# The second batch's phi softmax is moved ahead of the expert's pick, and its transposes go to other PSUM banks

## The chip, the cores and the metric

The kernel runs on one core of a Trainium2 chip. A core has a matrix engine (TensorE, PE in the profile, with its weight loads shown apart as PEld), a vector engine (VectorE, DVE), a scalar engine (ScalarE, ACT), GpSimd (POOL) and a sync engine (SyncE, SP) which here issues nearly all loads from HBM. Each engine takes its own instructions in the order in which the program lists them. The metric is the device time of one execution in microseconds (us), lower is better, and the median of the runs counts.

## The reference

Eight batches (B) of 576 tokens (S) with 8 heads (H) of 64 go through an attention in which keys and values are first gathered into 32 memory slots by a softmax over `phi`. The result is then sent through a mixture of 8 experts: each token picks one expert by a cosine with the expert's embedding.

```python
a = phi - np.max(phi, axis=2, keepdims=True)
a = np.exp(a)
a = a / (np.sum(a, axis=2, keepdims=True) + 1e-09)     # over the tokens
k_m = np.einsum('bhsm,bhsd->bhmd', a, k)
v_m = np.einsum('bhsm,bhsd->bhmd', a, v)
scores = scale * np.matmul(q, k_m.transpose(0, 1, 3, 2))
attn = softmax(scores)                                  # over the 32 slots
x = np.matmul(attn, v_m)                                # then (B*S, H*D)
...
expert_idx = np.argmax(xn @ en.T / tau, axis=1)
for e in range(E):
    mask = expert_idx == e
    h = np.maximum(x[mask] @ w1[e], 0.0)
    out[mask] = gate_w[mask, None] * (h @ w2[e])
```

## The kernel before

A batch has one expert for almost all of its tokens, so the kernel chooses one expert for the whole batch, loads its `w1` and `w2` and runs the 576 tokens through them as dense products; tokens with another expert would be done at the end. For batch 0 the expert is guessed early from the summed keys and values (`summed`, `guess`, `pick`), so that its weights can be loaded while the attention is still at work.

The function `moe_linformer` writes the start of the program out by hand: the attention of batch 0 and the gathering of batch 1 are mixed, line by line, and the order of these lines is the order in which each engine takes its instructions. Only then do the batches run in a loop (`batch`), whose stages `first` and `second` are the two products of the expert. A helper call such as `k.largest(1, 0)` therefore is at the same time a place in the queue of VectorE.

The 8 heads of a batch lie in two groups of four, g = 0 and g = 1. These are the steps around the change:

- `load_phi(1, (g,))` loads group g of batch 1's phi, 288 KB, into `ex`. SP issues it among the other loads.
- `largest(1, g)` (L509) takes the maximum over the tokens on VectorE, into `nm`. `softmax(1, (g,))` (L524) takes the exponential in place on ScalarE, with the sum in `sm`, and GpSimd copies the last 64 tokens apart (L526).
- `turn(1, g)` transposes four blocks of 128 tokens on TensorE into a PSUM tile `te` (L550) and copies them to `eT` on ScalarE (L551). `tails(1)` does the same with the last 64 tokens (`tz`, L557 and L558). `slots(1)` then multiplies `eT` with keys and values (`acc`, L607).
- `values(0)` transposes batch 0's values into a PSUM tile `tv` (L667) and copies them on ScalarE in four pieces (L673). `squares(0)` needs these copies; its result `tl` (L694) is copied by `products(0)` (L732).
- `score(0, tr, ...)` and `score(0, te, ...)` are batch 0's scores (`tr`, `te`, L686). VectorE transposes them into `x` (`fill`, L65), takes their maximum (`weigh`, L72) and subtracts it (L74, on GpSimd for g = 0), ScalarE takes the exponential (L76), VectorE sums (L85, `divide`), divides (L92) and transposes them back (L100, `aw`). With `aw` TensorE begins the attention's last product (`po`, L135), and from there the expert's first product (`pg`, L766, and `ph`, L791).
- `pick` (L227 to L231) reads the guess on VectorE and hands the expert's number to SP, which then issues the loads of `w1` (L494).

PSUM tiles come from named banks: `pt` takes the next of three in turn, `mm(..., n)` takes bank `m` with the number n. A new tile in a bank waits until the last reader of the tile before it is done. `warm` issues matmuls without use (`hot`, `warm0` to `warm2`), which keep TensorE at work.

Of the kernel before, what the change touches and what calls it, by code (L numbers as in the profile page):

```python
# [19 lines left out]
P = 128  # L20
# [27 lines left out]
class Tokens:  # L48
# [47 lines left out]
    def turn(self, gs, ks):  # L96

        k, nc, b = self.k, self.nc, self.b
        for g in gs:
            nc.vector.transpose(k.aw[:, g, 32 * ks.start : 32 * ks.stop], k.x[:, g, ks])  # L100
            if ks.stop == BL:
                nc.vector.transpose(k.aw[:, g, S:], k.x[:, g, BL - 2 :])  # L102
# [205 lines left out]
class Kernel:  # L308
# [234 lines left out]
        rs, g = self.room(b)[2], slice(gs[0], gs[-1] + 1)  # L543
        self.nc.vector.reciprocal(out=rs[:, g], in_=rs[:, g])

    def turn(self, b, g):

        t = self.pt([P, 4, P], f"te{b}_{g}")
        for k in range(4):
            self.nc.tensor.transpose(t[:, k], self.e(b, g)[:, P * k : P * k + P], self.ident)  # L550
        self.nc.scalar.copy(self.eT[:, 4 * g : 4 * g + 4], t)  # L551
# [558 lines left out]
@with_exitstack  # L1110
def moe_linformer(ctx, tc, phiT, qT, kv, kvt, emb, tau, w1, w2, out):
    k = Kernel(ctx, tc, phiT, qT, kv, kvt, emb, tau, w1, w2, out)
    ctx.enter_context(tc.manual_schedule(engines={ET.PE, ET.DVE, ET.Activation, ET.SP, ET.Pool}))


    k.eights()
    k.warm(8)
    k.warm(41, hot=k.mm([P, 64], "cool", 0))
    k.load_phi(0)
    k.load_kv(0)  # L1120
    k.load_q(0, (0,))
    k.load_router()
    k.consts()
    accs = [k.ps.tile([P, 2 * D], F32, tag=f"{n}3", name=f"acc0{n}", bufs=1) for n in "tm"]
    for vT in k.vT:
        k.nc.vector.memset(vT, 0.0)
    router = k.router()
    for g in range(NG):
        k.largest(0, g)
        k.softmax(0, (g,))  # L1130
    for g in range(NG):
        k.turn(0, g)
        if not g:
            next(router)
        k.warm(4 if g else 8, hot=k.mm([P, 256], f"half{g}", 0))
    k.tails(0)
    k.shares(0)
    next(router)
    k.load_phi(1, (0,))
    k.load_q(0, (1,))  # L1140
    k.load_phi(1, (1,))
    t = Tokens(k, 0, k.pt)
    for ks in ((0, 1), (4,), (2, 3)):
        k.slots(0, accs, ks=ks, first=0 in ks, last=3 in ks)
        if 3 not in ks:
            k.warm(3, hot=k.mm([P, 128], f"hot{ks[0]}", 0))
    k.scale(0)
    next(router, None)
    k.warm(2, hot=k.mm([P, 128], "hot2", 0))
    k.load_kv(1, (0,))  # L1150
    k.load_piece(1, 2)
    k.load_piece(1, 3)
    k.keys(0)
    t.summed()
    k.again()
    values = k.values(0, copy=k.nc.scalar.copy, room=lambda *a: k.mm(*a, 3))
    all, tr, te = slice(0, BL), [k.mm([P, S - 64], f"tr0_{g}", g) for g in range(NG)], [k.mm([P, 64], "te0_0", 2)]
    k.score(0, tr, 64, S, (0,))
    t.guess()
    k.score(0, te, 0, 64, (0,))  # L1160
    next(values)
    k.largest(1, 0)
    k.softmax(1, (0,))
    e = t.pick()
    t.fill((0,), slice(2, BL), tr)
    t.fill((0,), slice(0, 2), te)
    list(values)
    k.load_w1(e, 0)
    k.load_w1(e, 1)
    k.load_q(1, (0,))  # L1170
    tl = [k.pt([P, D + E], f"tl0_{g}") for g in range(NG)]
    k.squares(0, tl)
    k.score(0, tr, 64, S, (1,))
    te.append(k.pt([P, 64], "te0_1"))
    k.score(0, te, 0, 64, (1,))
    k.products(0, copy=True)
    k.largest(1, 1)
    work = [t.weigh((g,), all, None if g else k.nc.gpsimd) for g in range(NG)]
    for _ in range(2):
        next(work[0])  # L1180
    t.fill((1,), slice(2, BL), tr)
    t.fill((1,), slice(0, 2), te)
    k.softmax(1, (1,))
    k.turn(1, 0)
    k.warm(8, hot=k.mm([P, 256], "warm0", 3))
    k.turn(1, 1)
    list(work[0])
    for _ in range(2):
        next(work[1])
    list(work[1])  # L1190
    k.warm(8, hot=k.mm([P, 256], "warm1", 2))
    k.tails(1)
    k.shares(1, v=k.nc.gpsimd, invert=False)
    accs = [accs[0], k.mm([P, 2 * D], "acc1", 3)]
    for ks in ((0,), (1,), (2,), (4,), (3,)):
        k.slots(1, accs, ks=ks, first=0 in ks, last=3 in ks)
    project = k.project(0, k.vT[0], apart=True)
    t.divide(range(NG), all, True, lambda: k.invert(1))
    k.tags, k.turns = 4, 3
    k.scale(1)  # L1200
    k.again(k.nc.scalar.copy)
    t.turn(range(NG), all)
    for g in range(NG):
        k.part(g, slice(0, HS), k.nc.gpsimd.tensor_copy)
    k.warm(6, hot=k.mm([P, 256], "warm2", 2))
    k.keys(1, lambda *a: k.mm(*a, 3))
    list(k.values(1, copy=k.nc.scalar.copy, room=lambda *a: k.mm(*a, 2)))

    def between():
        for _ in range(3):  # L1210
            next(project)

    t.attend(between)
    t.turned(0, 1)
    t.turned(4)
    k.load_w2(e)
    k.load_q(1, (1,))
    k.load_phi(2)
    k.second_part = project
    for b in range(B):  # L1220
        u = Tokens(k, b + 1, k.pt) if b < B - 1 else None
        left = k.batch(b, t, u)
        t = u
    k.rest(*left)
# [29 lines left out]
```

## Time and profile before

| what | value |
|---|---|
| median of 3 runs | 391.76 us (389.92 to 392.36) |
| time of the profiled execution | 391.72 us |
| its span, first to last instruction | 389.9 us |
| TensorE busy (matmuls) | 383.0 us, 98% of the span |
| VectorE, ScalarE, GpSimd busy | 242.8, 213.3 and 190.1 us |
| mean granted TensorE clock | 0.999 |

The profile is of one execution; 1.8 us of its time lie outside of the span. All times in the views count from the start of the span. A busy matmul row counts its latency too, so that TensorE's share says little of where it waits; that is told by the weight loads (PEld), whose rows name an idle time and what ended it.

### The profile page before, as it was taken

To read this page: it belongs to the slowest core of one execution; us is meant where nothing else is said; L and a number is where in the kernel's file an instruction comes from. 1 tells how busy PE (TensorE), PEld (TensorE's weight loads), DVE (VectorE), ACT (ScalarE), POOL (GpSimd) and SP (SyncE) were. 2 spreads that over 40 slices of the span, in tenths; PEclk is the share of its full clock that TensorE was granted. 3 is DMA by queue.
4 is the path that set the end of the run, shared out by engine and by line. 5 is a ranking of instruction groups with operands and counts; after the bars stand their busy time and mean duration, and the time that the engine had idled before them with its cause. 6 is when DMAs were issued, how large, how long until landed. Compare 5 with 4: busy or idle time off the path is not lost. (4 is left out here: it accounts for less than half of the span.)

```text
span 389.9 us, 10386 instructions
## 1 busy us (share of the span) xinstructions
PE 383.0 (98%) x3881; PEld 313.5 (80%) x3881; DVE 242.8 (62%) x800; ACT 213.3 (55%) x665; POOL 190.1 (49%) x234
## 2 busy tenths in 40 slices
PE   8899999999999999999999999999999999999995
PEld 6578888798787978889787987879787897879883
DVE  4678996679663798259872798538861696545000
ACT  5466634868494865666657685657641751145011
POOL 1166930695155923378152941559242871529300
PEclk9999999999999999999999999999999999999999
DMA  8999938994699937994499917995379306970011
GB/s 314 397 358 349 366 78 228 346 389 156 161 315 375 379 72 167 400 380 174 91 310 366 402 34 168 345 386 209 65 185 382 127 2 130 322 306 2 30 54 44
DMA packets 65591, 91.25 MB, mean 234 GB/s; under 512 B 40728, under 2 KB 45336, under 8 KB 63488
## 3 DMA queue, kind: packets, MB, share of 16 engines
q1 hardware_dynamic: 62160, 81.02, 61.9%
q0 software_dynamic: 2688, 8.26, 5.7%
q10 hardware_dynamic: 688, 1.26, 1.1%
q8 instruction: 32, 0.52, 0.6%
q14 instruction: 23, 0.19, 0.1%
HBM read 71.19 MB, written 19.33 MB: 232 GB/s over the span
## 5 line engine op out<-in xcount | busy, mean ns | idle before, releaser
L791 PE MATMUL ph<-aT,gh 128*128 128x288 f32 x512 | 103.1, 296 | 0.0
L831 PE MATMUL py<-wh,hh 128*128 128x512 f32 x256 | 100.9, 394 | 0.0
L831 PE MATMUL py<-wl,hh 128*128 128x512 f32 x256 | 99.8, 390 | 0.0
L831 PE MATMUL py<-wh,hl 128*128 128x512 f32 x256 | 99.7, 389 | 0.0
L756 POOL TENSOR_TENSOR wl<-w2s,wh 128x512 fp32r<-128x512 f32 x64 | 83.3, 1302 | 5.1
L791 PEld LDWEIGHTS ph<-aT,gh 128*128 128x128 f32 x512 | 81.8, 188 | 1.9 <-DVE hl L798 0.8
L791 PE MATMUL ph<-aT,gl 128*128 128x288 f32 x256 | 75.4, 294 | 0.0
L795 ACT ACTIVATE hh<-ph 128x224 fp32r<-128x224 f32 (+1 forms) x128 | 48.7, 387 | 33.7 <-PE ph L791 33.0
L798 DVE SCALAR_TENSOR_TENSOR hl<-ph,hh 128x224 fp32r<-128x224 f32 (+1 forms) x128 | 51.8, 417 | 23.4 <-ACT hh L795 16.9
L997 POOL DMA_DIRECT2D out_dram<-ys x28 | 16.3, 582 | 91.2 <-ACT ys L836 88.9
L836 ACT ACTIVATE ys<-py,gate 128x512 f32<-128x512 f32 (+1 forms) x40 | 25.7, 643 | 63.7 <-PE py L831 33.9
L831 PEld LDWEIGHTS py<-wh,hh 128*128 128x128 f32 x256 | 48.1, 188 | 11.1 <-issue 1.4
L831 PEld LDWEIGHTS py<-wh,hl 128*128 128x128 f32 x256 | 48.1, 188 | 10.2
L831 PEld LDWEIGHTS py<-wl,hh 128*128 128x128 f32 x256 | 48.1, 188 | 9.4
L791 PEld LDWEIGHTS ph<-aT,gl 128*128 128x128 f32 x256 | 48.0, 188 | 0.0
L775 DVE TENSOR_TENSOR gl<-pg,gh 128x512 fp32r<-128x512 f32 x32 | 20.0, 683 | 43.9 <-ACT gh L771 43.9
L755 POOL CAST wh<-w2s 128x512 fp32r<-128x512 f32 x62 | 41.3, 666 | 0.1
L746 POOL TENSOR_TENSOR aT<-aw,aT 128x576 fp32r<-128x576 f32 (+1 forms) x18 | 23.5, 1319 | 32.7 <-DVE aT L745 29.2
L584 ACT COPY eT<-xt 32x256 f32<-32x256 f32 x80 | 32.3, 404 | 1.4
L820 PE MATMUL py<-w2s,h 128*64 128x256 f32 x256 | 29.4, 382 | 0.0
L656 ACT COPY kv<-kt 32x64 f32<-32x64 f32 x96 | 23.3, 243 | 6.4 <-DVE kt L646 5.2
L820 PEld LDWEIGHTS py<-w2s,h 128*64 128x64 f32 x256 | 17.7, 137 | 10.7 <-DVE aw L102 2.1
(184 smaller groups left out, 474.3 us busy)
## 6 DMA issues: line engine op xcount, KB each, us to landing
kx<-kv SPq DMA_DIRECT2D x15, 1024.0 KB, 12.0
w2s<-w SPq DMA_DIRECT2D x28, 512.0 KB, 10.0
w1s<-w SPq DMA_DIRECT2D x28, 512.0 KB, 5.8
qt<-qT SPq DMA_DIRECT2D x14, 576.0 KB, 10.2
out_dram<-ys POOLq DMA_DIRECT2D x28, 256.0 KB, 6.4
ad<-aw SPq DMA_DIRECT2D x8, 576.0 KB, 12.4
td<-x SPq DMA_DIRECT2D x56, 72.0 KB, 2.2
ea<-td SPq DMA_DIRECT2D x7, 512.0 KB, 4.2
```

The source lines that it names most:

```text
L584: nc.scalar.copy(eT[to, :8, m].rearrange("p (g k) m -> p g k m", g=NG), xt[at, :, q : BL - 2 : 4])
L656: nc.scalar.copy(y, self.kt[32 * l : 32 * l + 32, g, h + 2 * i :: 2 - 4 * i])
L746: self.nc.gpsimd.tensor_tensor(out=al, in0=a, in1=ah.bitcast(F32), op=ALU.subtract)
L755: (copy or self.nc.scalar.copy)(h, x)
L756: self.nc.gpsimd.tensor_tensor(out=l, in0=x, in1=h.bitcast(F32), op=ALU.subtract)
L775: nc.vector.tensor_tensor(out=self.gl[:, g, f], in0=ps[g], in1=self.gh[:, g, f].bitcast(F32), op=ALU.subtract)
L791: nc.tensor.matmul(p, lhsT=w[:, g, fs], rhs=x[:, g, to], start=g == 0 and k == 0, stop=g == 1 and k == 2)
L795: nc.scalar.activation(self.hh[:, f, at], q, AF.Relu)
L798: nc.vector.scalar_tensor_tensor(out=self.hl[:, f, at], in0=q, scalar=0.0, in1=self.hh[:, f, at].bitcast(F32), op0=ALU.max, op1=ALU.subtract)
L820: nc.tensor.matmul(p[64 * j : 64 * j + 64], lhsT=self.h4[:, f], rhs=self.w2s[:, f, d * j : d * j + d], start=f == 0, stop=f == 7,)
L831: nc.tensor.matmul(p, lhsT=h[:, f, to], rhs=w[:, f], start=f == 0 and k == 0, stop=f == 7 and k == 2)
L836: nc.scalar.activation(y[:, :d], p, AF.Copy, scale=gate[:, i : i + 1])
```

## The change

`largest(1, 0)` moves up to stand right behind `keys(0)`, ahead of `summed`; `largest(1, 1)` and both exponentials of batch 1 (`softmax(1)`) move ahead of `pick` and of the rest of `values(0)`, which holds the four copies. `turn(1, 0)` moves ahead of `squares(0)` and takes bank m3, where `tv` lies; `turn(1, 1)` takes bank m2. `tails(1)` moves ahead of the second half of `weigh`. The unused matmuls change: two groups of 8 with 256 columns become one group of 15 with 64 columns behind `tails(1)`, and the group of 6 with 256 columns ahead of `keys(1)` becomes 8 with 192 columns.

```diff
-    def turn(self, b, g):
+    def turn(self, b, g, room=None):
 
-        t = self.pt([P, 4, P], f"te{b}_{g}")
+        t = (room or self.pt)([P, 4, P], f"te{b}_{g}")
...
     k.keys(0)
+    k.largest(1, 0)
     t.summed()
...
     next(values)
-    k.largest(1, 0)
-    k.softmax(1, (0,))
+    k.largest(1, 1)
+    k.softmax(1)
     e = t.pick()
...
     k.load_q(1, (0,))
+    k.turn(1, 0, lambda *a: k.mm(*a, 3))
     tl = [k.pt([P, D + E], f"tl0_{g}") for g in range(NG)]
     k.squares(0, tl)
     k.score(0, tr, 64, S, (1,))
...
     k.products(0, copy=True)
-    k.largest(1, 1)
     work = [t.weigh((g,), all, None if g else k.nc.gpsimd) for g in range(NG)]
...
     t.fill((1,), slice(0, 2), te)
-    k.softmax(1, (1,))
-    k.turn(1, 0)
-    k.warm(8, hot=k.mm([P, 256], "warm0", 3))
-    k.turn(1, 1)
+    k.turn(1, 1, lambda *a: k.mm(*a, 2))
     list(work[0])
+    k.tails(1)
     for _ in range(2):
         next(work[1])
     list(work[1])
-    k.warm(8, hot=k.mm([P, 256], "warm1", 2))
-    k.tails(1)
+    k.warm(15, hot=k.mm([P, 64], "warm1", 3))
...
-    k.warm(6, hot=k.mm([P, 256], "warm2", 2))
+    k.warm(8, hot=k.mm([P, 192], "warm2", 2))
```

On VectorE, this is the stretch from the scaling of batch 0's keys and values (`ks<-acc0t`) to the first maximum of the scores (`mx0_00`), before the change. `nm1` are the maxima of batch 1, `key0` to `ai` is the pick.

```order
L626 TENSOR_SCALAR ks_75<-acc0t_186,rs0_192 128x128
L212 TENSOR_TENSOR ve_336<-kv21_79,key_331 128x32
L661 COPY ks_75<-ks_75 128x2x64
L509 TENSOR_REDUCE nm1_354<-ex_69 128x1
L227 TENSOR_REDUCE key0_363<-key_331 128x8
L228 MAX top_360<-key0_363 128x8
L229 MAX_INDEX at_361<-top_360,key0_363 128x8
L230 TENSOR_SCALAR ai_362<-at_361 128x1
L65 STREAM_TRANSPOSE x_81<-tr0_0_339 128x512
L65 STREAM_TRANSPOSE x_81<-te0_0_341 128x64
L509 TENSOR_REDUCE nm1_354<-ex_69 128x1
L72 TENSOR_REDUCE mx0_00_410<-x_81 128x18
```

The same stretch of VectorE after the change:

```order
L626 TENSOR_SCALAR ks_75<-acc0t_186,rs0_192 128x128
L509 TENSOR_REDUCE nm1_331<-ex_69 128x1
L212 TENSOR_TENSOR ve_340<-kv21_79,key_335 128x32
L661 COPY ks_75<-ks_75 128x2x64
L509 TENSOR_REDUCE nm1_331<-ex_69 128x1
L227 TENSOR_REDUCE key0_366<-key_335 128x8
L228 MAX top_363<-key0_366 128x8
L229 MAX_INDEX at_364<-top_363,key0_366 128x8
L230 TENSOR_SCALAR ai_365<-at_364 128x1
L65 STREAM_TRANSPOSE x_81<-tr0_0_343 128x512
L65 STREAM_TRANSPOSE x_81<-te0_0_345 128x64
L72 TENSOR_REDUCE mx0_00_418<-x_81 128x18
```

Group 0's maximum now stands ahead of `ve`, and group 1's maximum, which stood behind the pick and the first scores, stands ahead of both.

On TensorE, this is the stretch from the first scores of batch 0 (`tr0_0`) to the first transposes of batch 1's exponentials (`te1_0<-ident,ex`), before the change. `te0_0` and `te0_1` are the scores of the first 64 tokens, `tv0_0` the values, `tl0` the squares.

```order
L686 MATMUL tr0_0_339<-qt_73,kv20_78 32x512 x4
L218 MATMUL key_331<-ve_336,h4_95 128x32
L686 MATMUL te0_0_341<-qt_73,kv20_78 32x64 x4
L667 MATMUL tv0_0_351<-ident_166,ks_75 128x128 x2
L694 MATMUL tl0_0_386<-kv20_78 32x72 x4
L694 MATMUL tl0_1_387<-kv20_78 32x72 x4
L686 MATMUL tr0_1_340<-qt_73,kv20_78 32x512 x4
L686 MATMUL te0_1_400<-qt_73,kv20_78 32x64 x4
L550 MATMUL te1_0_417<-ident_166,ex_69 128x128 x4
```

The same stretch of TensorE after the change, up to the tails:

```order
L686 MATMUL tr0_0_343<-qt_73,kv20_78 32x512 x4
L218 MATMUL key_335<-ve_340,h4_95 128x32
L686 MATMUL te0_0_345<-qt_73,kv20_78 32x64 x4
L667 MATMUL tv0_0_355<-ident_166,ks_75 128x128 x2
L550 MATMUL te1_0_389<-ident_166,ex_69 128x128 x4
L694 MATMUL tl0_0_395<-kv20_78 32x72 x4
L694 MATMUL tl0_1_396<-kv20_78 32x72 x4
L686 MATMUL tr0_1_344<-qt_73,kv20_78 32x512 x4
L686 MATMUL te0_1_409<-qt_73,kv20_78 32x64 x4
L550 MATMUL te1_1_423<-ident_166,ex_69 128x128 x4
L557 MATMUL tz1_430<-ident_166,xt_83 128x128 x2
```

The transposes of batch 1's group 0 moved from behind the scores of group 1 (`tr0_1`, `te0_1`) to ahead of the squares. On ScalarE both exponentials (L524) now stand ahead of the four copies of the values (L673), where one stood before; the second stood behind the copies of the squares (L732).

## Rows read from the trace of the kernel before

**Rows 1.** The page: granted clock and DMA share in 40 slices of the span.

```profile
PEclk9999999999999999999999999999999999999999
DMA  8999938994699937994499917995379306970011
```

**Rows 2.** Timeline, TensorE and its weight loads: start, us, engine, line, tiles, [idle before <-releaser].

```profile
16.08 0.44 PE L667 MATMUL tv<-ident,ks 128*128 128x128 f32 x2
16.81 0.81 PEld L694 LDWEIGHTS tl<-kv 64*32 64x32 f32 x13 [0.53 <-ACT kv L673]
17.53 1.16 PE L686 MATMUL tr<-qt,kv 64*32 64x512 f32 x8
18.73 0.42 PEld L550 LDWEIGHTS te<-ident,ex 128*128 128x128 f32 x4
20.43 0.86 PEld L444 LDWEIGHTS <-ones 128*128 128x128 bf16 x8
21.72 0.43 PE L607 MATMUL acc0t<-kx,eT 128*32 128x128 f32 x8
25.70 0.71 PEld L135 LDWEIGHTS po<-vv,aw 64*64 64x64 f32 x40 [0.33 <-DVE aw L100]
39.84 0.40 PEld L694 LDWEIGHTS tl<-kv 64*32 64x32 f32 x16
```

**Rows 3.** Timeline, VectorE, 14 to 24 us.

```profile
14.69 0.19 DVE L212 TENSOR_TENSOR ve<-kv,key 128x32 f32<-128x32 f32 x1 [1.29 <-PE key L202]
...
14.94 0.75 DVE L509 TENSOR_REDUCE nm<-ex 128x1 f32<-128x576 f32 x1
15.95 0.19 DVE L227 TENSOR_REDUCE key<-key 128x8 f32<-128x32 f32 x1 [0.26 <-PE key L218]
...
17.48 0.71 DVE L509 TENSOR_REDUCE nm<-ex 128x1 f32<-128x576 f32 x1
18.11 0.74 DVE L72 TENSOR_REDUCE mx<-x 128x18 f32<-128x576 f32 x1
18.77 0.71 DVE L65 STREAM_TRANSPOSE x<-tr 128x512 f32<-128x512 f32 x1
...
20.43 0.76 DVE L74 TENSOR_TENSOR x<-x,mx 128x576 f32<-128x576 f32 x1
21.99 1.41 DVE L85 TENSOR_REDUCE z<-x 128x18 f32<-128x576 f32 x2 [0.81 <-ACT x L76]
```

**Rows 4.** Timeline, ScalarE, 15 to 25 us.

```profile
15.77 0.78 ACT L524 ACTIVATE ex<-ex,nm 128x576 f32<-128x576 f32 x1 [1.21 <-DVE nm L509]
...
16.56 0.90 ACT L673 COPY kv<-tv 64x64 f32<-64x64 f32 x4
...
21.27 1.26 ACT L76 ACTIVATE x<-x 128x576 f32<-128x576 f32 x2
...
24.16 0.37 ACT L624 ACTIVATE ks<-acc0t,rs 128x128 f32<-128x128 f32 x1 [1.36 <-PE acc L607]
```

**Rows 5.** Timeline, loads that SP issues, 7 to 19 us: start and time of the issue.

```profile
7.51 0.33 SPq L460 DMA_DIRECT2D ex<-phiT  x1
7.88 0.43 SPq L482 DMA_DIRECT2D qt<-qT  x1
8.81 0.33 SPq L460 DMA_DIRECT2D ex<-phiT  x1
10.47 0.33 SPq L472 DMA_DIRECT2D kx<-kv  x1
...
17.84 1.48 SPq L494 DMA_DIRECT2D w1s<-w  x2
```

**Rows 6.** DMA view, issues at 7.88, 10.47, 17.84: KB each, us from issue to landing.

```profile
qt<-qT SPq DMA_DIRECT2D x1, 576.0 KB, 8.0
...
kx<-kv SPq DMA_DIRECT2D x1, 1024.0 KB, 8.6
...
w1s<-w SPq DMA_DIRECT2D x1, 1024.0 KB, 7.3
```

## The prediction

> **What bounds the kernel now.** I read the page first. The granted clock is at its upper level in every slice and the DMA engines are full in the first slices [rows 1], while the table gives TensorE 98% of the span. From about 29 us on, TensorE is fed without a gap worth naming, so the change can move the time only by moving the moment at which that stretch begins. I therefore read the timelines of the first 30 us, engine by engine, and went back from the first attention product. Its weight loads begin at 25.70 and waited last for VectorE's `aw` [rows 2]. `aw` stands at the end of a run of VectorE work which starts with the sums `z` at 21.99 and goes on from 23.40, where the sums end (21.99 + 1.41), without a pause that the change touches [rows 3]. So the number to follow is **the end of the sums, 23.40 now**; what is added there is added to the whole.
>
> Before the sums VectorE waited 0.81 us for ScalarE's exponential [rows 3]. VectorE had done its last subtraction at 20.43 + 0.76 = 21.19, but the two exponentials started only at 21.27 and the second one about 0.63 later [rows 4]. They stand behind the copies of the transposes `te`, and these behind eight unused matmuls. There is slack to be won here: that is what the change takes away.
>
> **The gain, step by step.** With the transposes of batch 1 done early, the exponential of group 1 no longer queues; it follows the subtraction at once. The path from the subtraction's end to the end of the sums is then 0.08 (as from a maximum's end, 14.94 + 0.75, to its exponential at 15.77) + 0.72 (exponential to sum, 21.27 to 21.99) + 0.70 (one sum of two in 1.41) = 1.50 [rows 3, 4]. Now it is 23.40 - 21.19 = 2.21. **Gain: 0.71 us**, if the scores of group 1 come to VectorE as early as now, at 18.77 [rows 3].
>
> **The loss, step by step.** They don't, I think. The two maxima move ahead in VectorE's queue, and each needs its load of phi. For group 0 that is cheap: VectorE idles 1.29 us ahead of `ve` [rows 3], and a maximum takes 0.75. For group 1 it is not. Its load is issued at 8.81, behind a load of q (7.88) and ahead of one of kv (10.47) [rows 5]. The view of DMA issues gives no landing for phi itself, but it gives its neighbours': q at 7.88 + 8.0 = 15.9, kv at 10.47 + 8.6 = 19.1 [rows 5, 6]. If the queue is served in order, 288 of the 1312 KB that land in these 3.2 us are phi's, which puts it at 15.9 + 0.7 = **16.6**. The bounds are 15.9 (q's landing) and 17.48, where the old second maximum started without a wait for a DMA [rows 3]. I take 16.6, the value by the bytes, since DMA is full there [rows 1]. In the changed order the maximum is VectorE's next instruction from about 15 us on, so it would wait some 1.6 us for its data, and so would all that is queued behind it on VectorE: the pick, the first scores' transposes, their maximum.
>
> The longer way from there goes over ScalarE and TensorE. Let L be the start of group 1's maximum (16.6). Its exponential starts 0.83 later (14.94 to 15.77), the copies of the values 0.79 behind that (15.77 to 16.56) and end after 0.90 [rows 3, 4]. The transposes `te` of group 0 are now in the values' bank and wait for all four copies, where the squares `tl` used to begin when the first copies were there [rows 2]. They take 0.42; the squares behind them 0.40 (the undisturbed sixteen at 39.84; the ones at 16.81 were waiting between); the scores of group 1 take 1.16 from first to last, and VectorE starts 0.08 later (17.53 + 1.16 to 18.77) [rows 2, 3]. The sum is L + 4.58, so VectorE gets the scores of group 1 at 21.18 and not at 18.77: **2.41 us later**. From there 1.66 to the subtraction (18.77 to 20.43), its 0.76 [rows 3] and the 1.50 from above end the sums at 25.10. Against 23.40 this is a **net loss of 1.70 us**. As a formula the net is L - 14.90: the change pays only if phi is there when VectorE asks, and costs one microsecond for each that it is late.
>
> **What is hidden.** The pick moves with the maximum: it can start at L + 0.63 (17.48 to 18.11, one maximum to the next instruction) and not at 15.95, 1.3 later [rows 3], and the load of `w1` with it, from 17.84 to about 19.1. It lands 7.3 later, at 26.4 [rows 5, 6]; its product stands behind the first attention product, which moves to 25.70 + 1.70 = 27.40, so 1.0 us of cover is left. If that were gone, `w1` would be the last to come. GpSimd's two small copies and its sums of shares get earlier input than now or follow ScalarE, with no reader before the shares' reciprocal behind the sums. The unused matmuls: behind the scores (21.1 by the sum above) come the second transposes, 0.42, the tails, at most as long, and fifteen small ones, at most 0.86 / 8 each as the old wide ones, so 1.6 together. `acc` would start by 23.6 at the latest. Its sums took from 21.72 to less than 24.16, when ScalarE's scaling began [rows 2, 4], so they end by 26.0, just when VectorE has the scale ready (24.16 + 1.70 = 25.9). Thus they cost nothing, or 0.1 us at the worst. The eight in place of six ahead of the keys fall into TensorE's wait for that scaling.
>
> **Rivals.** First, **phi is early**. If group 1's phi has landed by 14.94, when VectorE has finished what stands ahead, the formula gives 14.94 - 14.90, about 0.0 us: 391.8. The dependence of `te` on all four copies eats the gain. For it speaks that phi is small and that loads run on 16 engines at once; against it that the three loads with a landing in the view landed in the order of issue, 15.9, 19.1 and 17.84 + 7.3 = 25.1 [rows 5, 6]. The Trainium skill, DMA: Bandwidth & Descriptors, section "Queues, rings and completion order", says that completion is not first-in first-out per issuing engine, so that a place between two neighbours is not proof; by it the time could be this rival's 391.8. The trace shows no overtaking, which leaves the rule a minor weight. I give this rival 0.27. A small gain also lies in it: if the squares and transposes overlap, 0.4 falls out of the 4.58 and the time is 391.4.
>
> Second, **TensorE's clock falls**, which would be clearly slower. Now TensorE has no idle time above 0.53 us in this stretch [rows 2], and the clock stays at 2.4 GHz [rows 1]. In my forecast it has nothing between the values' transposes (16.08 + 0.44 = 16.5) and `te` at 16.6 + 0.83 + 0.79 + 0.90 = 19.1, so 2.6 us, and the two groups of unused matmuls that filled such gaps are gone. If the clock went to 1.2 GHz through the sums `acc`, at most 2.4 us now, and through the first products from 25.70 to about 29, some 3.3 us, these would take up to twice as long; the first increase is half hidden behind VectorE, so I put 1.2 + 3.3 = 4.5 on top: 391.72 + 1.7 + 4.5 = 397.9. It decides from the point at which the gap is long enough. Against it stands that the trace has no fall at any gap, but also no gap like this one. The Trainium skill, TensorE: Matmul & The Clock Gate, section "HAM oscillation — how this bites in real kernels", tells of just this: bursts of matmuls with waits for data between them start again at the lower clock. No run here shows it yet. Chance 0.07.
>
> **How the numbers follow.** The profiled execution took 391.72, its span is 389.9, and the 1.8 around it stay; it stands 0.04 below the median of the runs shown, so no correction is due. Forecast: 391.72 + 1.70 = **393.4**, chance 0.62, with 392.7 to 394.3 for phi between 15.9 and 17.48. Phi early: 391.8, 0.27. Clock: 397.9, 0.07. Something that I don't see: 0.04. The range takes in the early phi and the upper end of the late one, each widened by 1.2, half of what the three runs differ by (392.36 - 389.92): 390.5 to 395.5. It leaves out the clock and the unseen.
>
> A measurement of this kernel tells about 1%, or 3.9 us, from no change; within that lie the forecast and the early phi. Faster by more has no mechanism here, 0.01; slower by more is the clock with a part of the unseen, 0.06; the same 0.93.
>
> **What the profile after would show.** Right: VectorE's second maximum waits for the DMA of phi and starts at 16 to 17 us; the pick behind it; the values' copies on ScalarE at about 18.2; TensorE idle until 19; the sums of scores ending near 25.1 and the first attention product near 27.4. Wrong: the second maximum at 14.9 with no wait, and the product near 25.7. The forecast fails if phi lands early, if TensorE's squares don't wait for the four copies, or if the granted clock shows a fall behind 17 us.

## The result and the profile after

The changed kernel takes 394.43 us, median of six runs (393.42 to 394.67), beside 391.91 of six runs of the kernel before (389.92 to 392.49). The ratio is 1.0066, with a 95% interval of 1.0040 to 1.0092: **slower by 2.5 us**, less than the 1% that the prediction called the bound, though the whole interval lies above 1. The profiled execution took 394.38 with a span of 392.6.

Nearly all of it is there when the first attention product begins: 28.24 us after, 25.70 before [rows 2], so 2.54 of the 2.66 us between the two profiled executions. From there to the end they take nearly the same (394.38 - 28.24 = 366.14, and 391.72 - 25.70 = 366.02). So I read the same stretch as for the prediction. One thing has to be kept in mind in it: two executions don't start alike. The transposes `tv`, which stand ahead of all that the change moves on TensorE, begin at 15.41 after and at 16.08 before, and between 13.95 and 16.18 in the fourteen traces of this case. From the first scores `tr` it is 1.58 to them after and 1.57 before, so the change itself didn't shift them.

First the page's granted clock and DMA share of the kernel after, to set beside [rows 1]:

```profile
PEclk9879999999999999999999999999999999999999
DMA  7999918995789936996479937996369306970011
```

The clock's second and third slices, 10 to 29 us, have fallen, where the kernel before has nines. Next VectorE's timeline of the kernel after, which answers to [rows 3]:

```profile
16.05 0.75 DVE L509 TENSOR_REDUCE nm<-ex 128x1 f32<-128x576 f32 x1 [1.23 <-DMA ex<-phiT]
16.72 0.18 DVE L227 TENSOR_REDUCE key<-key 128x8 f32<-128x32 f32 x1
...
21.87 0.72 DVE L65 STREAM_TRANSPOSE x<-tr 128x512 f32<-128x512 f32 x1 [2.76 <-PE tr L686]
...
23.54 0.76 DVE L74 TENSOR_TENSOR x<-x,mx 128x576 f32<-128x576 f32 x1
24.36 1.60 DVE L85 TENSOR_REDUCE z<-x 128x18 f32<-128x576 f32 x2
```

Group 1's maximum waits for phi, with the releaser named as the DMA, and starts at 16.05. The scores of group 1 are taken up at 21.87 and not at 18.77, after 2.76 us of waiting for TensorE. The sums no longer wait for ScalarE: the 0.81 of before is gone. They end at 25.96 instead of 23.40.

ScalarE's timeline, beside [rows 4], and TensorE's, beside [rows 2]:

```profile
16.89 0.77 ACT L524 ACTIVATE ex<-ex,nm 128x576 f32<-128x576 f32 x1 [1.34 <-DVE nm L509]
17.66 0.85 ACT L673 COPY kv<-tv 64x64 f32<-64x64 f32 x4
```

```profile
15.41 0.44 PE L667 MATMUL tv<-ident,ks 128*128 128x128 f32 x2
18.55 0.72 PEld L550 LDWEIGHTS te<-ident,ex 128*128 128x128 f32 x4 [2.95 <-ACT kv L673]
19.87 1.93 PE L686 MATMUL tr<-qt,kv 64*32 64x512 f32 x8
28.24 0.71 PEld L135 LDWEIGHTS po<-vv,aw 64*64 64x64 f32 x40 [0.33 <-DVE aw L100]
```

The chain is phi, maximum, exponential, four copies, `te`. TensorE has no weights to load for 2.95 us and comes back at the lower clock: `te` takes 0.72 where it took 0.42, the scores of group 1 take 1.93 where they took 1.16 [rows 2]. The view of windows of the kernel after shows the clock itself (columns: stretch, length, busy time of PE, PEld, DVE, ACT, POOL, granted clock, DMA share, GB/s):

```profile
17.10:20.50 3.40, 1.94 (x24) 1.18 (x28) 1.91 (x7) 2.10 (x9) 1.46 (x3) 0.56 0.91 355
20.50:23.90 3.40, 3.40 (x34) 2.28 (x27) 1.96 (x4) 1.36 (x5) 1.00 (x5) 0.50 0.98 355
23.90:27.30 3.40, 3.40 (x96) 3.02 (x93) 3.17 (x7) 1.87 (x5) 0.54 (x1) 0.94 1.00 371
```

0.50 is the lower level, 1.2 GHz. Of the six runs the profiled one alone shows the fall itself. The mean clock of the six runs is 0.991 to 0.996, and that of every run of the kernel before that was taken beside the experiments is 0.997 to 1.0, so it stands in nearly all of the six.

Last, the loads, beside [rows 5, 6]: the issues of q and of group 1's phi, and q's time to landing.

```profile
6.68 0.44 SPq L482 DMA_DIRECT2D qt<-qT  x1
7.61 0.33 SPq L460 DMA_DIRECT2D ex<-phiT  x1
```

```profile
qt<-qT SPq DMA_DIRECT2D x1, 576.0 KB, 8.6
```

q landed at 6.68 + 8.6 = 15.28, and the maximum that needs phi started 0.77 later.

### The profile page after: what moved, and what is told of

It is laid out like the page before. It is cut to its first block, busy times and chain, and to the rows that moved or that the text cites. A ratio compares the mean times of both kernels' runs of the same rounds, so it can differ in the third digit from the quotient of the medians.

```text
span 392.6 us, 10387 instructions
## 1 busy us (share of the span) xinstructions
PE 382.7 (97%) x3882; PEld 312.6 (80%) x3882; DVE 243.1 (62%) x800; ACT 213.2 (54%) x665; POOL 189.9 (48%) x234
## 5 line engine op out<-in xcount | busy, mean ns | idle before, releaser
L798 DVE SCALAR_TENSOR_TENSOR hl<-ph,hh 128x224 fp32r<-128x224 f32 (+1 forms) x128 | 51.8, 417 | 23.3 <-ACT hh L795 16.9
```

The lines of the kernel that those rows point to most:

```text
L798: nc.vector.scalar_tensor_tensor(out=self.hl[:, f, at], in0=q, scalar=0.0, in1=self.hh[:, f, at].bitcast(F32), op0=ALU.max, op1=ALU.subtract)
```

## The experiments

Unless another base is named, a diff is against the changed kernel. One number for each, called the rest, tells how long the kernel took behind the start: the profiled execution's time less the start of its first attention product (366.0 before).

**1. TensorE kept busy in the wait** (e1_fill): 24 unused products between the transposes of the values and those of the exponentials.

```
     next(values)
+    k.warm(24, hot=tr[1][:, :256])
     k.largest(1, 1)
```

> The changed kernel with 24 unused matmuls of 256 columns put between the values' transposes and the transposes of batch 1, in a bank that the scores overwrite later. They fill 24 x 0.107 = 2.6 us of TensorE's idle 2.95 us and wait for nothing. If the fall of the clock (from 17.5 to 24.3 us in the changed kernel) is a cost of its own, the granted clock comes back to 0.999, the scores of group 1 take 1.16 again where they took 1.93, the transposes of group 0 0.42 to the next weight load where they took 1.05, and the time falls by some 1.3 us, from 394.4 to 393.1. If only the wait for phi and what stands behind it counts, the time stays at 394.4 whatever the clock does.

Measured: 394.29 us (393.61 to 395.65), ratio 1.0074 [1.0049, 1.0099]: no gain. Yet the clock stayed up (0.996 to 1.0 in its runs) and the first attention product came at 26.34, 1.9 earlier than in the changed kernel. So the start was better and the time was not: 394.75 - 26.34 = 368.41, which is 2.4 more than the kernel before needs from there. Part of it stands at the second batch's first expert product, which waited for its weights:

```profile
77.78 0.19 PEld L766 LDWEIGHTS pg<-w1s,kv 64*32 64x32 f32 x16 [1.14 <-DMA w1s<-w]
```

One trace doesn't tell whether that was chance or the kernel's own.

**2. The same, once more** (e1_again).

> The kernel with 24 unused products of 256 columns once more, for its trace alone. If the wait of 1.14 us for the second batch's weights near 78 us belongs to the kernel, it stands there again, with SyncE's issue of that load near 67 us; if it was a chance, the first attention product is again near 26.3 us and the span is about 1.3 us under 392.9.

Measured: 394.75 us; phi came late (maximum at 16.66), the product at 27.25, and 394.75 - 27.25 = 367.50. The wait for the weights shrank to 0.21, so that one was not fixed in the kernel:

```profile
77.75 0.20 PEld L766 LDWEIGHTS pg<-w1s,kv 64*32 64x32 f32 x8 [0.21 <-DMA w1s<-w]
```

The rest is 1.5 too long all the same. This time most of it is lost at the very end, where the last stores of the output land in 2.4 and 2.6 us instead of 2.0 and 2.2. So a loss behind the first product stands in both traces of this kernel, but not at one place. Experiments 6 and 9 to 12 take this up.

**3. Only the transposes back** (e2_turn_back): `turn(1, 0)` behind the products again.

```
-    k.turn(1, 0, lambda *a: k.mm(*a, 3))
     tl = [k.pt([P, D + E], f"tl0_{g}") for g in range(NG)]
...
     k.products(0, copy=True)
+    k.turn(1, 0, lambda *a: k.mm(*a, 3))
```

> The changed kernel with the transposes of batch 1's group 0 back behind the scores of group 1; all else stays, the late phi and the gap too. If the transposes and their wait for all four copies stand on the way to the scores, the squares begin with the first two copies (0.4 us earlier) and the scores lose the 1.05 us of the transposes: 1.3 us less, 393.1. If the scores were late for another reason (the clock, the load of q), 394.4.

Measured: 394.12 us (393.42 to 395.76), ratio 1.0070 [1.0043, 1.0097], the clock down as in the changed kernel. From TensorE's and VectorE's timelines:

```profile
17.94 0.83 PEld L694 LDWEIGHTS tl<-kv 64*32 64x32 f32 x13 [3.78 <-ACT kv L673]
...
20.94 1.57 PEld L550 LDWEIGHTS te<-ident,ex 128*128 128x128 f32 x8 [0.17 <-PE tr L686]
```

```profile
20.85 0.72 DVE L65 STREAM_TRANSPOSE x<-tr 128x512 f32<-128x512 f32 x1 [1.71 <-PE tr L686]
...
24.20 0.75 DVE L85 TENSOR_REDUCE z<-x 128x18 f32<-128x576 f32 x1 [0.92 <-ACT x L76]
```

The scores reach VectorE 1.02 earlier than in the changed kernel, but all eight transposes run late at the lower clock, ScalarE's copies of them hold the exponentials, and the sums wait for these again. The first product is at 28.09. The transposes' place is not what costs.

**4. Group 1's maximum and exponential back** (e3_max1_back).

```
-    k.largest(1, 1)
-    k.softmax(1)
+    k.softmax(1, (0,))
...
     k.products(0, copy=True)
+    k.largest(1, 1)
...
+    k.softmax(1, (1,))
     k.turn(1, 1, lambda *a: k.mm(*a, 2))
```

> The changed kernel with group 1's maximum and exponential alone put back to their old places, behind the first scores' transposes; the transposes keep their new place and banks, and the unused matmuls their new number. If the wait of VectorE for group 1's phi is the root, the pick starts at once, the values' copies follow the first exponential at about 15.5, TensorE's gap shrinks to about 1 us, the clock doesn't fall, and the sums of scores end near 22.5 and not at 26.0: 3.5 us less, 390.9, faster than the kernel before. If the new place of the transposes or the fewer unused matmuls are the root, it stays above 393.

Measured: 392.25 us (391.34 to 393.16), ratio 1.0018 [1.0003, 1.0034]. Most of the loss is gone with this one step (the ratio was 1.0066), and with it the fall of the clock: eleven of the twelve runs have a mean clock of 0.997 to 1.0, one has 0.994. The gain didn't appear: the late exponential now holds the second transposes, and the sums wait 0.72 for ScalarE.

```profile
20.60 0.42 PEld L550 LDWEIGHTS te<-ident,ex 128*128 128x128 f32 x4 [1.31 <-ACT ex L524]
```

```profile
22.55 1.59 DVE L85 TENSOR_REDUCE z<-x 128x18 f32<-128x576 f32 x2 [0.72 <-ACT x L76]
```

**5. Phi's load ahead of q's second half** (e5_phi_first), everything else as changed.

```
     k.load_phi(1, (0,))
-    k.load_q(0, (1,))
     k.load_phi(1, (1,))
+    k.load_q(0, (1,))
```

> The changed kernel with the load of batch 1's second phi issued ahead of the second half of q (576 KB) and not behind it. If the place in the load queue sets the landing, phi comes 576 KB earlier, some 1.4 us, so that VectorE's second maximum starts near 14.9 and waits for little. The gap on TensorE shrinks to some 1.8 us. Without a fall of the clock the time is then 392.0 (1.2 us from the wait, 1.2 from the clock), with it 393.3. If loads land in no order, nothing changes: 394.4.

Measured: 391.77 us (389.96 to 393.63), ratio 1.0013 [0.9991, 1.0034]. The wait is gone (below, VectorE), `te` follows after a gap of 1.58, and the clock stays up in this execution; the first product is at 26.01. Of the twelve runs three have a mean clock of 0.993 to 0.995, and they are the three slowest.

```profile
15.42 0.75 DVE L509 TENSOR_REDUCE nm<-ex 128x1 f32<-128x576 f32 x1
...
19.79 0.72 DVE L65 STREAM_TRANSPOSE x<-tr 128x512 f32<-128x512 f32 x1 [1.32 <-PE tr L686]
...
21.46 0.76 DVE L74 TENSOR_TENSOR x<-x,mx 128x576 f32<-128x576 f32 x1
22.13 1.59 DVE L85 TENSOR_REDUCE z<-x 128x18 f32<-128x576 f32 x2
```

So without the wait the change is worth about nothing. The prediction's formula has this: it pays only from a maximum at 14.9.

**6. The same columns in half the products** (e6_fill512).

```
     next(values)
+    k.warm(12, hot=tr[1])
     k.largest(1, 1)
```

> The changed kernel with 12 unused products of 512 columns between the transposes of the values and those of the scores: the same unused columns as the 24 products of 256, in half the instructions. The products of 256 had brought the first attention product from 28.24 us to 26.34, and yet the time stayed at 394.29, because the second batch's first product waited 1.14 us more for its weights near 78 us and 0.4 more were lost at 195. Theory A (the late start is the whole cost, and that slip was a chance or the price of 24 more instructions in the way of SyncE's issue): first attention product near 26.3, nothing lost behind it, 392.4 to 393.0. Theory B (a later point makes up for whatever the start gains or loses, so the clock and the wait are worth nothing at the end): 394.0 to 394.6 again, with the same wait for weights near 78 us.

Measured: 393.83 us (392.62 to 395.45), ratio 1.0078 [1.0055, 1.0102]. Neither theory's number: theory A's start, but a time between the two. The profiled execution was the fastest of the six: maximum at 15.81, product at 26.40, and 392.62 - 26.40 = 366.22, nothing lost behind it. SyncE's wait for the stores of batch 1's weights, 1.6 us before, was 3.0 all the same; here it fell on no reader. What the other five runs lost against this one isn't placed.

**7. Only the second exponential back** (e7_exp1_back); the maximum stays ahead.

```
-    k.softmax(1)
+    k.softmax(1, (0,))
...
     k.products(0, copy=True)
+    k.softmax(1, (1,))
```

> The changed kernel with only the second exponential put back behind the products of the first half; the second maximum still stands ahead of the pick. Theory A (VectorE's wait for phi is what costs, and ScalarE's second exponential ahead of the four copies only adds to it): the maximum still ends near 16.8 us, the pick near 16.9, the copies start near 17.1 instead of 17.66, the scores' transposes run some 0.6 to 0.8 earlier, the clock may still fall; the exponentials of the attention weights wait for the late second exponential, so that the first attention product is at 27.0 to 28.0 and the time 393.2 to 394.2. Theory B (ScalarE's queue is the link, VectorE's wait is covered): copies near 16.6, first attention product at 26.4 or earlier, 392.3 or less.

Measured: 393.01 us (391.43 to 393.83), ratio 1.0044 [1.0029, 1.0059], between the two theories. Phi came latest of all here:

```profile
16.85 0.75 DVE L509 TENSOR_REDUCE nm<-ex 128x1 f32<-128x576 f32 x1 [1.17 <-DMA ex<-phiT]
```

```profile
17.57 0.42 PEld L550 LDWEIGHTS te<-ident,ex 128*128 128x128 f32 x4 [1.19 <-ACT kv L673]
...
26.63 0.71 PEld L135 LDWEIGHTS po<-vv,aw 64*64 64x64 f32 x40 [0.33 <-DVE aw L100]
```

With ScalarE free for the copies, TensorE's gap is 1.19 and the clock stays; what remains is VectorE's own queue behind the maximum. So the loss has two parts: VectorE's wait, and the gap on TensorE that ScalarE's second exponential opens.

**8. Phi first, the gap filled, the transposes back** (e9_best): the edits of 3 and 5, eight unused products of 256 columns in the wait, and the weights of group 0 (`list(work[0])`) ahead of `turn(1, 1)`, the tails behind `work[1]`.

> The changed kernel with the second phi loaded ahead of q's second half, eight unused products of 256 columns in the wait, and the first half's scores back behind its products, with the second half's weight products spread out. Theory A (phi's landing was the cost, and with it gone the earlier exponentials bring what they should): maximum without a wait near 15.4, scores' sums end near 23.2, first attention product 25.5 to 25.7, 391.0 to 391.4, at or just under the kernel before. Rival (the chain of copies and transposes holds the scores however early phi is): first attention product at 26 or later, 391.8 or more.

Measured: 392.00 us (391.26 to 392.83), ratio 1.0020 [1.0005, 1.0036], with the first product at 23.97, 1.73 earlier than before. Of this, 1.00 is the early front of this execution, whose `tv` began at 15.08 and not at 16.08:

```profile
15.08 0.20 PEld L667 LDWEIGHTS tv<-ident,ks 128*128 128x128 f32 x2
...
23.97 0.71 PEld L135 LDWEIGHTS po<-vv,aw 64*64 64x64 f32 x40 [0.34 <-DVE aw L100]
```

From `tv` to the product it takes 8.89 and the kernel before 9.62 (25.70 - 16.08), so the kernel's own gain at the start is 0.73. The median lost 0.6 all the same, for the rest is 1.6 longer: 391.61 - 23.97 = 367.64. Here too the second batch's first expert product waits 0.84 for its weights.

**9. As many products as the changed kernel** (e10_even): experiment 6, with two later groups of unused products cast into half as many, twice as wide.

```
+    k.warm(12, hot=tr[1])
...
-    k.warm(15, hot=k.mm([P, 64], "warm1", 3))
+    k.warm(7, hot=k.mm([P, 128], "warm1", 3))
...
-    k.warm(8, hot=k.mm([P, 192], "warm2", 2))
+    k.warm(4, hot=k.mm([P, 384], "warm2", 2))
```

> The changed kernel with 12 unused products of 512 columns in the wait, and the two later groups of unused products cast into half as many of twice the width (15 of 64 columns into 7 of 128, 8 of 192 into 4 of 384): as many products in all as the changed kernel had, and their columns more. In the traces with 12 or 24 products more, a 16 KB load of instructions falls into the middle of the 36 us long way from the second batch's weights through DRAM: eight stores that take 5.3 us in the kernel before and 5.4 in the changed one take 6.5 to 7.5 there. Theory A (TensorE's clock costs 1.2 to 1.9 us here, and only that load of instructions took it back): stores back at 5.3 to 5.5 us, first attention product near 26.3, 392.0 to 392.8. Theory B (the clock is worth nothing at the end): 393.6 to 394.4 with the stores at 5.4.

Measured: 393.48 us (392.60 to 394.96), ratio 1.0048 [1.0025, 1.0071], over what theory A wanted and under theory B. The trace has phi late at 16.49, the clock up, and a rest of 393.15 - 27.08 = 366.07, the same as before. VectorE, then TensorE's weight loads, then the windows:

```profile
16.49 0.75 DVE L509 TENSOR_REDUCE nm<-ex 128x1 f32<-128x576 f32 x1 [1.16 <-DMA ex<-phiT]
...
20.86 0.72 DVE L65 STREAM_TRANSPOSE x<-tr 128x512 f32<-128x512 f32 x1 [1.32 <-PE tr L686]
```

```profile
16.10 2.37 PEld L444 LDWEIGHTS <-ones 128*128 128x128 bf16 x12
18.99 0.42 PEld L550 LDWEIGHTS te<-ident,ex 128*128 128x128 f32 x4 [0.53 <-ACT kv L673]
...
27.08 0.71 PEld L135 LDWEIGHTS po<-vv,aw 64*64 64x64 f32 x40 [0.33 <-DVE aw L100]
```

```profile
15.00:20.00 5.00, 4.97 (x52) 2.52 (x52) 3.25 (x12) 2.71 (x9) 0.85 (x3) 1.00 0.95 367
```

This is the changed kernel with its wait and without its clock fall: from the maximum to the first product 27.08 - 16.49 = 10.59. In e1_fill (26.34 - 15.74 = 10.60), e1_again, e5_phi_first and e6_fill512 (10.59 each) it is the same; in the changed kernel it is 28.24 - 16.05 = 12.19. **The clock costs 1.60 us at the first attention product.**

**10. Only the count of products, in the kernel before** (e11_count; diff against the kernel before).

```
-    k.warm(8, hot=k.mm([P, 256], "warm0", 3))
+    k.warm(20, hot=k.mm([P, 104], "warm0", 3))
...
-    k.warm(8, hot=k.mm([P, 256], "warm1", 2))
+    k.warm(20, hot=k.mm([P, 104], "warm1", 2))
```

> The kernel before, with two of its groups of unused products cut finer (8 of 256 columns into 20 of 104, twice): 24 products more, about the same columns and the same time in their place. Theory A (the number of TensorE's instructions decides when the 16 KB of instructions are loaded, and that load delays the second batch's stores): first attention product at 25.7 as before, stores 6.5 to 7.5 us instead of 5.3, a wait for the second batch's weights near 78 us, time 392.2 to 393.2. Theory B (the longer stores of the other runs came from something else): 391.2 to 391.6, nothing to tell from before.

Measured: 393.47 us (392.11 to 396.81), ratio 1.0064 [1.0041, 1.0087]. Cutting unused work finer costs 2.0 us, most of what the whole change costs, although each group took only 1.03 us in place of 0.86 [rows 2]. The stores took 6.0 us (54.6 to 60.6 us), less than theory A said, and SyncE waited 2.6 for them; no reader waited near 78 us. The profiled execution was the fastest of the twelve. Its first product came at 23.62, 2.08 early, because its whole front was early:

```profile
13.95 0.20 PEld L667 LDWEIGHTS tv<-ident,ks 128*128 128x128 f32 x2
...
23.62 0.71 PEld L135 LDWEIGHTS po<-vv,aw 64*64 64x64 f32 x40 [0.23 <-DVE aw L100]
```

From `tv` to the product it takes 9.67, where the kernel before takes 9.62, so the finer groups cost 0.05 there. Of the 2.08, 1.5 went in a pause of TensorE that ends at 29.30 and to which the trace puts no releaser. A second trace of the kernel follows.

**11. The same, once more** (e11_again).

> The kernel before with 24 products more by finer cutting, once more for its trace: the execution seen first was the fastest of twelve (392.11 us against a median of 393.47), with stores of 5.98 us and a start that came 2.08 us early. If the load of instructions in the stores is what costs, an execution near 393.5 us shows stores of 6.5 us or more, and a second batch's first product that waits for its weights. If it shows 5.3 to 5.5 us of stores, the cost lies elsewhere.

Measured: 392.18 us, against 390.55 of the kernel before in the run beside it. First product at 24.90, 0.80 earlier than in the trace of before and again 9.67 behind its `tv` (15.23), and a rest of 367.28. The pause that ended at 29.30 isn't there. The stores (6.0 us, a wait of 2.7) again delay no reader. The loss stands at two other places. One is a pause of TensorE inside a group of 16 equal weight loads, with no releaser named. They take 0.78 us, in the kernel before 0.18. TensorE's weight loads of before, then of e11_again:

```profile
194.51 0.18 PEld L607 LDWEIGHTS acc<-kl,eT 64*32 64x32 f32 x16 [0.20 <-issue]
```

```profile
193.75 0.15 PEld L607 LDWEIGHTS acc<-kl,eT 64*32 64x32 f32 x8 [0.20 <-issue]
194.38 0.15 PEld L607 LDWEIGHTS acc<-kl,eT 64*32 64x32 f32 x8 [0.47 <-issue]
```

The other is the very end, shown below under hardware. So theory A of experiment 10 is right that more products cost time, and wrong on where it is paid.

**12. Experiment 8 with as many products as the changed kernel** (e12_best_even): 15 unused products of 64 columns cast into 7 of 128.

> The version with phi first, eight unused products in the wait and the scores back behind the products, with 15 unused products of 64 columns cast into 7 of 128, so that it has as many products as the changed kernel. Theory A (its 392.0 was the load of instructions in the stores: they took 6.4 us, and the 1.73 us won at the first attention product were 0.41 behind the second batch's first product): stores 5.3 to 5.5 us, 390.6 to 391.2, at or under the kernel before. Theory B (what is won at the first attention product is lost behind it however the instructions lie, by the chain of stores and loads through DRAM): 391.7 to 392.2.

Measured: **391.11 us** (390.25 to 391.96), ratio 0.9988 [0.9973, 1.0002]: 0.9 under experiment 8 by this alone, and at the kernel before or a little under it. SyncE's wait is back at 1.6 us, no reader waits for weights near 78, the first product is at 24.97, 9.34 behind its `tv` (15.63), and the rest is 391.06 - 24.97 = 366.09.

## Why the prediction's range held, and where its steps were off

**The forecast's mechanism** holds at every step it named. VectorE's maximum waits for phi, the pick follows it, the copies, `te`, squares and scores follow in that order, and each 1 us of phi is 1 us of the first product's start: with the clock up that start is 10.59 or 10.60 behind the maximum in five traces, whenever phi comes. The measured time, 394.4, lies 1.0 above the 393.4 forecast and in the range, but just above the 394.3 that was the upper end for a late phi alone. And the forecast's last sign of failing came true: the granted clock fell behind 17 us. So the nearness of the number is in part luck, since errors in both directions met: of the forecast loss of 1.70, phi took off 0.55 by landing at 16.05 and not at 16.6, and the path 0.21 by being shorter, while the clock put 1.60 on, which makes the 2.54 at the first product.

**L, the landing of phi.** Forecast 16.6, measured 16.05 in the profiled execution. In the seven traces with phi's load in its place and the maximum ahead of the pick (after and six experiments) it lies between 15.74 and 16.85, with a mean of 16.24. The step by bytes (0.7 behind q) was good: 0.77 here. By the Trainium skill, DMA: Bandwidth & Descriptors, section "Queues, rings and completion order", phi need not have kept its place; in these seven traces VectorE waited for it until 15.7 us or later, so the rival of an early phi didn't happen. What an early phi gives was right as well: the rival said no change, and experiment 5 shows a ratio of 1.0013 [0.9991, 1.0034], with phi at 15.42 and not quite at the rival's 14.94.

**The path behind L.** L + 4.58 was forecast for the scores at VectorE. It is 4.37 with the clock up (20.86 - 16.49 in experiment 9, 19.79 - 15.42 in 5), so 0.21 too much; the squares and the scores overlap. It is 21.87 - 16.05 = 5.82 in the changed kernel. From L to the first product the forecast was 27.40 - 16.6 = 10.80; with the clock up it is 10.59. So the point from which the change pays is 25.70 - 10.59 = 15.11, not 14.90. And the loss at the first product is (16.05 - 15.11) for phi, 0.94, and 1.60 for the clock, together 2.54. Both counts are for the front of the profiled execution of before. The point lies 0.97 ahead of its `tv` and moves with it. Counted from `tv`, the first product is 12.83 away after (28.24 - 15.41) and 9.62 before, so in these two executions the change cost 3.21, and 0.67 of that was covered by the earlier front; the medians differ by 2.5.

**The gain of 0.71** is real. In the changed kernel the exponential no longer queues, and with the clock up the sums end 1.50 behind the subtraction, as forecast: in experiment 5, 22.13 + 1.59 less 21.46 + 0.76. It is inside the formula and is eaten by the path.

**The clock** is the step that failed in size and chance. I priced it at 4.5 us on top and gave it 0.07; it fell in the profiled execution, by the mean clocks in nearly all of the six runs, and cost 1.60. The price was wrong in its terms: it was 1.2 for the sums `acc` and 3.3 for the first products, and the windows show the clock up again soon behind 24 us, when `acc` had just begun (24.22) and ahead of the products. What ran at the lower clock were the transposes, the squares and the scores, which the price left out. The chance was too low because I read "no fall at any gap" from a trace whose longest gap behind `tv` was 0.53 [rows 2]. The gap itself I had as 2.6; it is 2.71 between the products and 2.95 between their weight loads. The Trainium skill, TensorE: Matmul & The Clock Gate, section "HAM oscillation — how this bites in real kernels", describes this, short bursts with a wait for data between them that restart at the lower clock; the trace agrees, with 0.50 to 0.56 granted from 17.1 to 23.9 us. A gap of 1.58 (experiment 5, profiled execution) and of 1.19 (4, 7) had no fall.

**What was hidden** stayed hidden: `w1`, issued at 18.61, delays no product, and the first attention product still waits for VectorE's `aw` and not for the keys.

**What stays open.** By the traces the clock is worth 1.60 at the first product. That it is worth as much at the end isn't shown: by the medians, 394.43 against 393.48 of experiment 9, it is about 1.0, by the ratios 0.7, and the two intervals overlap; experiments 1 and 6, with the clock up but more products, were no faster than the changed kernel. Phi's landing differs by 1.1 us from one execution to the next and the front by 2.2, so single traces don't settle the last half microsecond. Of experiment 10's 2.0 us, the second trace shows 0.6 in the pause and 0.7 at the end; what is left isn't placed.

## What to carry to other kernels

An instruction moved ahead in an engine's queue brings its load with it: look up when that load lands, and work out from which landing the move pays (here 15.11 us in the profiled execution of before, with phi at 15.7 to 16.9). Compare two traces from a point that the change doesn't touch (here `tv`), since the front differed by up to 2.2 us from one execution to another. A move that opens a gap on TensorE like the 2.95 us here needs the clock in its sum, at the price of what runs until the clock is back and no more. And when unused products are added or cut, hold their number: at about the same columns, more products moved this kernel by 0.9 and by 2.0 us, so an experiment that adds instructions needs a twin with the old count.

## What the runs showed of the hardware

**Loads of instructions share the DMA engines with data.** The page before has a queue "q8 instruction" with 32 packets and 0.52 MB, so 16 KB each. With more products on TensorE its packets come at other moments, and in six traces one falls among the eight stores that take batch 1's weights to DRAM (`td<-x`). The DMA view of that stretch, first of the kernel before (55.2 to 60.5 us; no q8 packet, the next one comes between 60.5 and 61, as the last store lands), then of e1_fill (55.8 to 62.9):

```profile
td<-x SPq DMA_DIRECT2D x6, 72.0 KB, 2.1
```

```profile
q8 instruction: 1, 0.02, 1.0%
...
td<-x SPq DMA_DIRECT2D x7, 72.0 KB, 3.0
```

1.0% of 16 engines' 7.1 us is 1.1 us for that one packet. SyncE's wait for the last store, from the view of its waits, first before, then e1_fill, then e9_best:

```profile
SPq L112 <- DMA td<-x: 1.6, 1, 1.6
```

```profile
SPq L112 <- DMA td<-x: 2.8, 1, 2.8
```

```profile
SPq L112 <- DMA td<-x: 3.3, 1, 3.3
```

It is 2.6 to 3.3 in every trace with the packet among the stores (e1_fill, e1_again, e6_fill512, e9_best, e11_count, e11_again) and 1.6 in all the others. Behind it SyncE issues the second batch's weights, which is how e1_fill and e9_best came to wait for these (1.14 and 0.84), while e6_fill512, e11_count and e11_again lost nothing by it. The last stores of the output show the same. The DMA view of 385.7 to 388.6 us, of e11_again:

```profile
q8 instruction: 1, 0.02, 2.6%
...
out_dram<-ys SPq DMA_DIRECT2D x1, 64.0 KB, 2.7
out_dram<-ys ACTq DMA_DIRECT2D x1, 64.0 KB, 2.9
```

Before, with no such packet there, these land in 2.0 and 2.2 us:

```profile
out_dram<-ys SPq DMA_DIRECT2D x1, 64.0 KB, 2.0
out_dram<-ys ACTq DMA_DIRECT2D x1, 64.0 KB, 2.2
```

That the packet itself delays the stores is read from this coincidence and from two pairs of kernels that differ in the number of products (before and 10; 8 and 12); a packet moved by itself wasn't tried. The Trainium skill, Runtime: NRT & Kernel Launch, section "Instruction fetch mechanics", says that instructions are streamed in 16 KiB blocks over a DMA queue of the engine's own and that this is mostly hidden. The trace agrees on the size; in these six traces the stores beside a block took longer, and in three of them TensorE then waited for weights (1.14, 0.84 and 0.21).
